# Attention and expert layers on one core: the last group's outputs expert by expert, part of the softmax inversions on GpSimd, and a new written order

## The chip, the cores and the metric

The kernel runs on one core of a Trainium2 chip. The core has five engines that work at the same time and each take their own instructions in program order: PE (TensorE, matrix products), DVE (VectorE), ACT (ScalarE), POOL (GpSimd) and SP (SyncE, which here only starts transfers). The metric is the device time of one execution in microseconds (us); lower is better.

## What is computed

Four batches of 1088 rows go through two layers. The first is a linear attention with sketched features: queries and keys (4 heads, 32 wide) are multiplied by two small random matrices, the outer product of the two sketches is the feature row, and the output is a ratio of two sums over the keys. Its output, four heads side by side, is the 128-wide input `x` of the second layer, four attention experts of which each row picks two:

```python
logits = x @ w_gate                      # 4 experts, the best 2 are kept
w = softmax over the two chosen logits
for e in range(E):
    scores = scale * (x @ wq[e]) @ (x @ wk[e]).T      # causal
    a = exp(scores - max); a /= a.sum(-1) + 1e-09
    ye = a @ (x @ wv[e]) @ wo[e]
    out += (expert e chosen for this row) * w * ye
```

All of it is float32, and the result must be the reference's.

## The kernel before, in words

**Tiles and stages.** A batch's 1088 rows are 17 blocks of 64 rows (index `i`), in three groups (`groups`, line 141): blocks 0 to 5, 6 to 11 and 12 to 16, so 384, 384 and 320 rows. As each row has two chosen experts, a block of 64 rows has 128 rows of scores. `prepare(b)` makes a batch's `x`: sketches (L518), their turn back on DVE (`back`, L522), products of sketches (`features`, one job for each head, on DVE or POOL, L527), sums over keys (L558), and from these `x`, twice: turned (`xT`) and as rows (`xra`, `xrb`, `xrc`, by way of DRAM). `choose_experts(b)` makes the masks of the chosen experts, also by way of DRAM.

For each group `queries` (L960, L969, L973) projects `x` for all four experts and picks the chosen ones by mask. For each block `scores` (lines 987 to 1054) runs a chain over four engines: PE multiplies (`score`, L998), DVE takes the scores with the causal mask and the row maximum (`take`, L1010), ACT exponentiates and adds up each row (`exp`, L1026), ACT or POOL adds 1e-9 to the sum (`guard`, L1032 or L1034), DVE inverts the 128 sums, one number in each partition (`invert`, L1037), POOL multiplies the block by the inverse and by the expert's share (`weigh`, L1041), DVE turns the block in squares of 32 (`turn A`, L1046). There are 68 such blocks. `values` (L1074) then sums over the keys for a whole group on PE, in two pairs of PSUM banks; the results are copied four times into `agg` (`keep V`, ACT or DVE), two of the copies are patched by mask (`patch V`, L1097, DVE), and POOL multiplies them by the masks in two instructions of two experts each (`spread V`, L1101). `outputs` projects `agg` with `Mo`: piece by piece of 128 rows, four experts for each piece (`project`, L1144), one copy to SBUF (`keep out`) and one store (L1157) for groups 0 and 1; all at once, turned (L1124, L1127) and stored in four transfers (L1130) for group 2.

**What sets the order.** Every such step is a job: a name, the engines it may run on with a price for each in us, what it reads, makes and holds. `ORDER` is a list of job numbers, written out; a letter behind a number picks the first (a, or none) or the second (b) engine of a job. `Plan.run` issues the jobs in just that order, so `ORDER` fixes the order on every engine and on the queues of the transfers, and, as buffers are taken from their pools in that order, also which buffer each tile gets. A job `dummy` multiplies a constant twice (L247) into a free pair of banks and feeds nothing; of 40 such jobs 6 are run, the others are left out. The last batch takes its groups in the order 1, 2, 0, so group 0 of batch 3 is the last work of the kernel.

PSUM is four pairs of banks (`ps`). `copy(eng, ...)`, line 191, is the line of every copy, whichever job makes it; in the profile such rows are told apart by their tiles and shapes.

Of the kernel before, what the change touches and what calls it, by code (L numbers as in the profile page):

```python
# [14 lines left out]
ALU = mybir.AluOpType  # L15
# [6 lines left out]
56 45 47 0 1 8a 77 60 46 3 2 76 25a 19a 17a 48 79 49 51 78 57 90 89 74 87 75 88 50 13b 98 100 99 102a 103a 91 92 83 93  # L22
97a 84 81 104b 22a 101b 113 96a 117 118a 82 111 112a 115 109 110a 94a 95a 38b 80 392 86 85 106 116a 393 114a 105 108a
107a 391 394 402 395 401 405 406 119 404 408a 54 120 124 125 129 407 130 121 66 122a 52 64 58 53 65 146 131 410a 126
411a 67b 132a 400 127a 147 152 55 68 397 396 69 123 71 150 70 148 153 155 44b 398 180 72 27b 16b 684 149 151 167 168
169 170 63 156 157a 158 685 159a 59 409b 179 184a 183a 154 162 163 181 399 185 73 182 413 412 186 414a 61 403 174 687
686 695 694 416 194 62a 415 417 195 196 420b 418b 215 216 419b 217 218a 421 222 423 9b 24b 31b 26b 422 164 219 171 128
165 137 187 188 133 172 246 173 430 431 197a 198 223 424 425 189 190a 191 245 250a 12b 166a 199 688 249a 201 202 200
318 5b 432 160 203 208 175 251 7a 426 427a 433a 224 247 192 428b 248 225a 161a 209 429 434a 210 252 319 322a 323a 193
435 698 268 226 227 700 699 204a 205 206 139 220 135 176 267 269 270 228 436 438a 207 141 703a 271b 704b 437b 324 221  # L30
211a 212 260 261 262 263a 213 275 321 276 277 278 279b 177 178b 214 253 254 456 458 272 457 273 14b 142 693 320 325
255 292 291 293 274 701a 42b 264 691 280 702a 134 136 229 230 231 459 460 692 256b 234a 284 294 283 233a 462 281 257
232a 258 265 690 689 706 705 285 286 235b 342 707a 708 237 236 239 709 710 696 713a 238 711a 712a 259 282 697 461 266
295a 296 343 326 344 297 287a 327 328 288 289 298 714 715 717 463 350 290 329 330b 716 723 724 725 345 346a 10b 143
21b 472 138 331 473 477b 718 347 351 352 35b 353 354a 144 727a 332 348 719 140 29b 439 476b 464 299 300 301 302 303
304 308a 441 306a 307a 726a 333 349 467 478 335 310 474 440 334 305b 309 475 336 479 359 337 338a 358 360 339 361 362
355 468 508 509 442 720a 984 311 312 540 721a 363 340 501 364a 443 502 480 979 341 481 482 541 314 465 487 365 488 356
357 483a 315 313 366 367 538 494 977 978 495 980 316a 981 728 539 542a 368 369 370 987 496 503 504a 145 371 372 373
374 317 469 375 470 543a 544 545 471a 505 506 985 988 484 485 486 497b 444 498 722 499 510 511b 489 490a 491 512 513
376 379b 447 500 380a 515 383 516 553 377a 381 445 554 492 493 378a 382 448 584 585 586 517 518a 729 555 449 446 453  # L40
982 983 730a 514 519 731b 451 991 520 521 993 749 556b 992 994b 587 588a 569 546 996b 750 384 385 997a 507 557 558 547
751 548 386 568 989 522 589 523 524 549a 550 551 559 570 571 526a 752 753 590 242 591 525a 754 611 529 995a 530 241
528b 527a 531 612 616a 561 760 732 452 387 615a 755 455 466 733 572a 756 560 573 574 389 614 562 563 986 613 240 576
577 617 618 620 575 43b 552 532 644 28b 18b 619 578 579 621 243a 580b 581 643 765 652 564a 565 766 769a 582 651 768
757 645 583 636 566 567 390 653 770a 771 635 654 655 627 622 244 623a 761 762 628 637 656 657b 629 630 638 767 772 624
658 659 646 625 592 660 639a 640 631b 641 593 594 450 595 596 597 794 598a 999 647a 632 642 601b 602 648 600a 599a 795
633 634 649 998 736 1000a 603 605 535 626 454 773 774 787 650 534 763 788 533 780 781 808 809 810 811a 764a 536b 812
661 662 789 775 663 813 796 797b 798 790b 604 782 664 665 666 667 1002 814 668 669 990 1005a 734 776b 777 672a 671a
778 1006b 670b 1001 735 739 1003 832 1004a 791 388 799 783b 800 673a 674 675 831 835a 801 784 1007 802 803 1008 792
676 1009 793 836a 834 677 1010 1016 833 904 738 678 742 30b 758 804b 1011 837 1017 785 805 806 759 1012 1018 838 1013a  # L50
905 908a 862 1014a 1020a 909a 807 679 910 878 786 779 737 537 877 879 747 839 840 841 907 906 880 911 861 863 1019a
1021 881b 842a 846 847 682 740 815 816 817 746 864 865a 820a 853 866 867 821a 824 854 1015 868 882 936 819a 823 39b
34b 40b 41b 855 848 849b 937 818a 850 851 856 822 938 1022 1024b 869 1023b 607 843 883 884 939 870 748 871 872 1042
857b 1044 928 680 741 681 844 845 1043 858 606 873a 874 929 608 1045 825 1047 852 930 940a 1046 1048 875 859 860 921
944 945 946 920 743 941 609a 922 610 744 913 931 932a 1049 912 914 947 933 934 942 915 948 876 949 950b 1126 916a 917
951 1125 1053 918 1054 1124 1128b 935 1025 1127 923 952 885 886 943 887 888 889 890 1129a 1051 891a 1130 1131 892b
924a 925 894b 895 828 896 926 898 893a 33b 927 32b 826 953 827 1139 829a 830 4 1147 1140 919 897 1055 1146 1132 1133
1148 1154 1155 1156 1198 1199 1149 1150a 1197 1201a 1134 1052 1027 1141 1142b 1143 1200 954 955 956 957 958 959 1202a
745 1029 1028 1026 1035 683 1037 960 1056 1057b 1135b 1157 1158b 1159 961 962 1203 1204 1213 1136 1137 1170 963a 1144
1145 1160 966a 1161 1171 1214 964a 968 1151 1152 1138 965a 967 1237 1205 1206 1172 1173 1174a 1238 1229 1215 970 969  # L60
1031 1207 1208 1209a 1239 1216 1059 1153 1039 1230 1162 1163 1217a 1240 1058 1231 1164 1061 1210 1211 1165 1241 1060
1063b 1050 1218 1062b 1166b 971 1064 1167 1175 1232 1242 899 1212 972 1168 1065 1176 1177 6b 1233a 1234 1169 1221
1243b 1040 1244 1222 1223 901 1235 1224 1066 900 1038 1067 1068 1245 1246 1219 1033 1069b 902a 1032 1030 1220 1101
1102 973 1178 1179 1034 1087 1225b 1226 1227 1236 1073 1074 1180 1075 1228 1088 1076a 1036 1181 1080 1081 1077 1094
1095 1096 1182 1103 1104b 1183 1184b 1097b 1098 1186b 1089 1090b 1091 1247 1248 1249 976 1187a 1105 1106 1250 1251
1252 1041 1188 1253 1254 1255 1185b 1189 1092 11b 1190 23b 903 1107 36b 1191 1194 1078 1070 1082 1083a 1193 1099 1093
975 1084 1071 1257b 1100 974 1192 1258a 1256a 1079 1085 1260 1261 1263 1259b 1086 1262 1072 1108 1195a 1196 1109 1110
1113a 1114b 1111a 1112b 1116 1117 1115 1264 1265 1267 1268 1266 1118 1120 1119 1121 1122a 15b 1269 1123 37b 20b
# [46 lines left out]
def kernel(  # L115
# [35 lines left out]
    def const(name, shape, dt=F32):  # L151
        return cp.tile(shape, dt, name=name, tag=name)
# [40 lines left out]
    def d_us(n):  # L193
        return 0.18 + n / 960

    def a_us(n):
        return 0.2 + 0.00073 * n

    def p_us(n):
        return 0.12 + 0.0022 * n  # L200
# [16 lines left out]
    warm = const("warm", [128, 1])  # L217
    den = const("den", [128, 2, 12])
# [16 lines left out]
    def first():  # L235
        nc.vector.memset(room(0, 64), 0)
        nc.vector.memset(warm, 0.0)

# [708 lines left out]
    def masks_of(b, n, *xs):  # L947
        return [("mb", b, n, x) for x in xs] if b == 0 and n == 0 else [("mb", b, n, 0)]
# [38 lines left out]
    def scores(b, n, i, rank):  # L987
# [48 lines left out]
        def invert():  # L1036
            nc.vector.reciprocal(rs[:, b, i : i + 1], rs[:, b, i : i + 1])  # L1037
# [13 lines left out]
        job(f"invert {b}.{i}", "DVE", 0.153, lambda e: invert(), [("zg", b, i)], ("r", b, i), rank=rank)  # L1051
# [4 lines left out]
    def values(b, n, rank):  # L1056
# [46 lines left out]
        r = rank + 0.1  # L1103
        for x in (2, 3, 0, 1):
            job(f"keep V {b}.{n}.{x}", ("ACT", "DVE"), (a_us(w), d_us(w)), lambda e, x=x: keep(e, x),
                [("V", b, n)], ("aggk", b, n, x), [Vk[x % 2], agg], rank=r)
# [3 lines left out]
        for x in range(2):  # L1110
            need = [("aggk", b, n, 0), ("aggk", b, n, 1)] if x == 0 else [("aggp", b, n)]
            job(f"spread V {b}.{n}.{x}", "POOL", p_us(2 * w), lambda e, x=x: spread_sums(x),
                [*need, *masks_of(b, n, x)], ("agg", b, n), [agg, mb], rank=r)

    def outputs(b, n, rank):
# [4 lines left out]
        if w % 128:  # L1120
# [15 lines left out]
            for g in range(4):  # L1136
                job(f"store out {b}.{n}.{g}", "SP", 0.5, lambda e, g=g: store_columns(g), [("ob", b, n)], None, [ob],
                    landing=0.35, rank=rank + 0.01)
            return
# [94 lines left out]
```

## Time and profile before

| | us |
|---|---|
| median of 3 runs | 280.45 |
| lowest and highest | 280.03, 280.90 |
| the profiled execution, as a run | 280.91 |
| its span, first to last instruction | 279.2 |
| around the span | 1.71 |
| busy: PE, DVE, POOL, ACT | 263.8, 218.8, 153.3, 100.2 |

The profile is one execution. Each row of a view is a group of instructions: the line, engine and operation, the tiles written and read with their shapes, how many, and their times. A float32 product of 128 x 128 weights is two records on PE, so 12 products are 24 rows. In the view by stretches of time, the numbers behind the stretch are the busy us of PE, PE's weight loads, DVE, ACT and POOL, then the granted PE clock (1.00 is full). In the timeline, `[5.76 <-issue]` is the time for which the engine stood idle before the row, and what ended it. The chain of work that ended last is followed back from the end: each piece is what the end was waiting for at that time.

### The profile page before, as it was taken

How to read it: one execution, taken by the hardware profiler on the slowest of the kernel's cores; microseconds unless marked ns; L12 is line 12 of the kernel's file. 1: busy time of each engine (PE TensorE's matmuls, PEld its weight loads, DVE VectorE, ACT ScalarE, POOL GpSimd, SP SyncE). 2: the span in 40 equal slices, each digit the busy share in tenths (PEclk: the TensorE clock that was granted, in tenths of full speed). 3: DMA queues.
4: the chain of work that ended last, by engine and by line, in shares of the span. 5: the costliest groups of instructions: out<-in, count | busy, mean ns of one | idle time of the engine just before them, and what ended most of it. 6: DMA issues, size and time to landing. Idle time of an engine off the chain costs nothing.

```text
span 279.2 us, 9471 instructions
## 1 busy us (share of the span) xinstructions
PE 263.8 (94%) x3953; PEld 194.8 (70%) x3953; DVE 218.8 (78%) x541; ACT 100.2 (36%) x272; POOL 153.3 (55%) x246
## 2 busy tenths in 40 slices
PE   5789899899999999989999999999999999999993
PEld 1478575448486796676589976756696975789973
DVE  4895998999989987998969437999898468986340
ACT  2030346254333444433462331463423335233110
POOL 6323636677789834546565458655447432544570
PEclk9979999999999999999999999999999999999999
DMA  8855749921617879243900166701403756820012
GB/s 179 139 141 102 112 124 258 153 34 24 143 32 120 166 184 180 57 102 65 198 6 4 30 150 141 162 2 38 108 2 76 130 116 133 165 56 5 2 31 52
DMA packets 85547, 27.36 MB, mean 98 GB/s; under 512 B 54080, under 2 KB 84864, under 8 KB 85504
## 3 DMA queue, kind: packets, MB, share of 16 engines
q1 hardware_dynamic: 83280, 26.47, 46.4%
q8 instruction: 31, 0.51, 0.8%
q10 hardware_dynamic: 2224, 0.28, 0.6%
q14 instruction: 12, 0.10, 0.1%
HBM read 22.22 MB, written 4.52 MB: 96 GB/s over the span
## 4 chain that ended last, share of the span: by engine, by line
PE 70%; DVE 20%; issue 5%; POOL 2%; ACT 1%; DMA 1%; DVEq 0%; POOLq 0%
PE pair L1074 24%; PE pair L998 19%; PE pair L960 9%; PE pair L1144 6%; PE pair L518 3%; PE pair L558 3%; DVE AT L1046 2%; DVE w L522 2%; DVE w L1010 2%; DVE fp L527 2%; PE pair L1124 2%; PE pair L615 1%; PE pair L592 1%; DVE in L494 1%; DVE xT L191 1%
## 5 line engine op out<-in xcount | busy, mean ns | idle before, releaser
L1041 POOL TENSOR_SCALAR w<-w,rs,sh 128x384 f32<-128x384 f32 (+15 forms) x68 | 55.6, 824 | 54.8 <-DVE rs L1037 52.0
L998 PE MATMUL pair<-xT,qs 128*128 128x384 f32 (+11 forms) x216 | 76.8, 482 | 1.7 <-DVE agg L191 1.3
L1026 ACT ACTIVATE w<-w,mx 128x640 f32<-128x640 f32 (+15 forms) x68 | 52.4, 770 | 72.3 <-DVE mx L1010 56.6
L998 PEld LDWEIGHTS pair<-xT,qs 128*128 128x128 f32 x216 | 37.7, 190 | 26.9 <-issue 10.0
L1046 DVE STREAM_TRANSPOSE AT<-w 128x576 f32<-128x576 f32 (+13 forms) x68 | 50.6, 758 | 5.4 <-POOL w L1041 5.2
L1010 DVE CUSTOM_DVE_ANT_0 w<-pair,mask 128x768 f32<-128x768 f32 (+13 forms) x68 | 48.3, 721 | 5.4 <-PE pair L998 4.7
L1074 PEld LDWEIGHTS pair<-AT,xra 32*128 32x128 f32 x1136 | 41.6, 185 | 6.0 <-DVE mx L1010 2.6
L1074 PE MATMUL pair<-AT,xra 32*128 32x192 f32 (+5 forms) x1136 | 44.5, 303 | 0.0
L1101 POOL TENSOR_TENSOR agg<-agg,mb 128x768 f32<-128x768 f32 (+1 forms) x24 | 37.3, 1565 | 12.7 <-ACT agg L191 6.6
L960 PE MATMUL pair<-xT,Mq 128*128 128x384 f32 (+1 forms) x96 | 34.9, 478 | 0.1
L527 POOL TENSOR_TENSOR fp<-w 128x576 f32<-128x576 f32 x21 | 25.4, 1224 | 14.2 <-DVE w L522 12.5
L191 ACT COPY agg<-pair 128x384 f32<-128x384 f32 (+1 forms) x33 | 14.0, 462 | 44.2 <-PE pair L1074 37.7
L1074 PE MATMUL pair<-AT,xrb 32*128 32x160 f32 (+5 forms) x752 | 26.9, 287 | 0.3 <-issue 0.3
L1074 PEld LDWEIGHTS pair<-AT,xrb 32*128 32x128 f32 x752 | 26.1, 186 | 1.0 <-issue 1.0
L1144 PEld LDWEIGHTS pair<-Mo,agg 128*128 128x128 f32 x192 | 23.4, 192 | 4.1 <-POOL agg L1101 1.7
L1144 PE MATMUL pair<-Mo,agg 128*128 128x128 f32 x192 | 24.9, 279 | 1.0 <-POOL agg L1101 0.9
L960 PEld LDWEIGHTS pair<-xT,Mq 128*128 128x128 f32 x96 | 17.2, 190 | 11.2 <-issue 3.2
L973 DVE COPY_PREDICATED qs<-mb,pair 128x768 f32<-128x768 uint16 (+1 forms) x24 | 23.0, 960 | 2.4 <-DMA mb<-md 1.8
L191 DVE COPY agg<-pair 128x384 f32<-128x384 f32 (+1 forms) x15 | 7.9, 532 | 13.1 <-PE pair L1074 11.7
L518 PE MATMUL pair<-in,SK 32*32 32x288 f32 x416 | 13.4, 494 | 3.0 <-DVE in L494 3.0
L522 DVE STREAM_TRANSPOSE w<-pair 128x576 f32<-128x576 f32 x16 | 11.6, 756 | 5.6 <-PE pair L518 5.6
L1097 DVE COPY_PREDICATED agg<-mb,pair 128x384 f32<-128x384 uint16 (+1 forms) x24 | 12.6, 550 | 3.3 <-ACT agg L191 2.9
(160 smaller groups left out, 295.4 us busy)
## 6 DMA issues: line engine op xcount, KB each, us to landing
mb<-md SPq DMA_DIRECT2D x7, 576.0 KB, 5.2
xra<-xd SPq DMA_DIRECT2D x16, 192.0 KB, 4.3
xrb<-xd SPq DMA_DIRECT2D x16, 192.0 KB, 3.6
xrc<-xd SPq DMA_DIRECT2D x16, 160.0 KB, 4.9
mb<-md SPq DMA_DIRECT2D x4, 480.0 KB, 5.4
in<-in_k_dram SPq DMA_DIRECT2D x12, 136.0 KB, 4.1
in<-in_q_dram SPq DMA_DIRECT2D x3, 544.0 KB, 5.5
xd<-w SPq DMA_DIRECT2D x12, 136.0 KB, 3.5
```

The costliest lines, as they stand in the source:

```text
L191: (nc.scalar.copy if eng == "ACT" else VEC[eng].tensor_copy)(o, i)
L527: VEC[e].tensor_tensor(out=f, in0=a[:, :, None, R : 2 * R].to_broadcast([128, NJ, R, R]), in1=a[:, :, 0:R, None].to_broadcast([128, NJ, R, ...
L960: nc.tensor.matmul(plan[ps[x]][:, y, 0:w], Mq[:, ((1, 2), (0, 3))[x][y]], plan[xT][:, 64 * t0 : 64 * t1], start=True, stop=True)
L973: nc.vector.copy_predicated(chosen(), rows(c), rows(plan[ps[x]]))
L998: nc.tensor.matmul(plan[p][:, y, 0 : c1 - c0], plan[qs][:, 128 * t : 128 * t + 128], plan[xT][:, c0:c1], start=True, stop=True)
L1010: nc.vector.tensor_tensor_reduce(out=o, in0=src, in1=msk, scale=-1.0, scalar=mx[:, b, i, x - 1 : x] if x else 3e38, op0=ALU.add, op1=ALU.m ...
L1026: nc.scalar.activation(out=a, in_=a, func=ACTF.Exp, bias=mx[:, b, i, last : last + 1], scale=-1.0, accum_out=zs[:, b, i : i + 1])
L1041: nc.gpsimd.tensor_scalar(out=a, in0=a, scalar1=rs[:, b, i : i + 1], scalar2=plan[("sh", b)][:, i : i + 1], op0=ALU.mult, op1=ALU.mult)
L1046: nc.vector.transpose(dst[:, 0 : keys // 32, t], plan[A][:, 0:keys].rearrange("p (j s) -> p j s", s=32))
L1074: nc.tensor.matmul(plan[Vk[g // 2]][:, g % 2, lo : 32 * nt], plan[(f"xr{j // 12}", b)][rows, j % 12], a[rows, j, lo:], start=(j == 0), sto ...
L1101: nc.gpsimd.tensor_tensor(out=a, in0=a, in1=plan[mb][:, 2 * x : 2 * x + 2, 0:w], op=ALU.mult)
L1144: nc.tensor.matmul(plan[p][0:m, 0, 128 * x : 128 * x + 128], plan[agg][:, e, 128 * x : 128 * x + m], Mo[:, e], start=(e == 0), stop=(e == ...
```

## The change

**The order.** `ORDER` is replaced as a whole by another list, with other choices of engine. The jobs are the same but for those below. Counted in the two lists, these move between engines:

| job | before | after |
|---|---|---|
| invert (softmax, 68) | DVE 68 | DVE 31, POOL 37 |
| features of queries | DVE 3, POOL 13 | DVE 9, POOL 7 |
| features of keys | DVE 8, POOL 8 | DVE 6, POOL 10 |
| base (copies of queries) | ACT 19, DVE 5 | ACT 16, DVE 8 |
| keep x (copies of x) | ACT 5, DVE 4 | ACT 8, DVE 1 |
| guard | ACT 39, POOL 29 | ACT 41, POOL 27 |
| keep V | ACT 33, DVE 15 | ACT 29, DVE 17 |
| keep w | DVE | ACT |
| scale of shares | POOL 3, DVE 2 | POOL 1, DVE 4 |

Of the six dummy jobs, four stood ahead of the first sketch, one behind the second sketch and one among the first batch's queries; in the new list one stands between the two first sketches, one among the first batch's later work and four behind the last output. On DVE, the first instructions `room` and `idle` change places.

**The inversion on POOL** is a new choice for the same job: the sum to the power of -1, with a constant tile `minus`. The plan's price for it is 0.555 us, against 0.153 us on DVE.

**The last group** (batch 3, group 0) gets its own jobs. `keep V` is left for two copies of four; the two others become `mix V`, in which DVE multiplies the PSUM sums by the mask straight into `agg`. The two-expert multiplications of POOL become one for each patched expert (`scale V`, POOL or DVE; the new list has one on each). The outputs are projected expert by expert, in the order 0, 2, 1, 3, three pieces for each, into three banks; each piece has its own copy and its own store, the stores from SP's or ACT's queue.

```diff
+    minus = const("minus", [128, 1])
...
         nc.vector.memset(warm, 0.0)
+        nc.vector.memset(minus, -1.0)
...
-        def invert():
-            nc.vector.reciprocal(rs[:, b, i : i + 1], rs[:, b, i : i + 1])
+        def invert(e):
+            r = rs[:, b, i : i + 1]
+            if e == "DVE":
+                nc.vector.reciprocal(r, r)
+            else:
+                nc.gpsimd.tensor_tensor(out=r, in0=r, in1=minus, op=ALU.pow)
...
-        job(f"invert {b}.{i}", "DVE", 0.153, ...)
+        job(f"invert {b}.{i}", ("DVE", "POOL"), (0.153, 0.555), ...)
...
+        if last_group(b, n):
+            def mix(x):
+                nc.vector.tensor_tensor(out=by_half(plan[agg][:, x]), in0=sums_of(x), in1=by_half(plan[mb][:, x]), op=ALU.mult)
+            def scale_one(e, x):
+                a = plan[agg][:, 2 + x, 0:w]
+                VEC[e].tensor_tensor(out=a, in0=a, in1=plan[mb][:, 2 + x, 0:w], op=ALU.mult)
+            for x in range(2):
+                job(f"keep V {b}.{n}.{2 + x}", ("ACT", "DVE"), ...)
+                job(f"mix V {b}.{n}.{x}", "DVE", ...)
+                job(f"patch V {b}.{n}.{x}", "DVE", ...)
+                job(f"scale V {b}.{n}.{x}", ("POOL", "DVE"), ...)
+            return
...
+    def last_group(b, n):
+        return b == B - 1 and n == 0
...
+        if last_group(b, n):
+            ps = [("ps", "po", b, n, x) for x in range(2)]
+            def piece(x):
+                return plan[ps[x // 2]][:, x % 2, 0:128]
+            def project_expert(e, first_, last_):
+                for x in range(3):
+                    nc.tensor.matmul(piece(x), plan[agg][:, e, 128 * x : 128 * x + 128], Mo[:, e], start=first_, stop=last_)
+            def keep_piece(e, x):
+                copy(e, plan[ob][:, 128 * x : 128 * x + 128], piece(x))
+            def store_piece(e, x):
+                (nc.scalar if e == "ACT" else nc.sync).dma_start(out=..., in_=plan[ob][:, 128 * x : 128 * x + 128])
+            order = (0, 2, 1, 3)
+            for y, e in enumerate(order):
+                job(f"out {b}.{n}.{e}", "PE", 12 * 0.056, ..., [("agg", b, n, e), ("M", 1)] + ([("po", b, n, y - 1)] if y else []), ...)
+            for x in range(3):
+                job(f"keep out {b}.{n}.{x}", ("ACT", "DVE"), ...)
+                job(f"store out {b}.{n}.{x}", ("SP", "ACT"), (0.45, 0.45), ...)
+            return
```

On the engines, the end of the new order reads: DVE keep V 2, patch 0, mix 0, mix 1, patch 1, turn out of group 2, scale 1, keep out 0, keep out 1; ACT keep V 3, keep out 2, store 2, store 0; POOL scale 0; PE out of group 2, then experts 0, 2, 1, 3, then the four dummy jobs; SP four stores of group 2, store 1.

114 lines of the change are left out of this document (66 added, 48 removed).

## The prediction

> **What bounds the kernel now.** I read the page first, then the stretches of time, then the end of the timeline, then single prices. The page says who is busy and what the end waited for:
>
> ```profile
> PE 263.8 (94%) x3953; PEld 194.8 (70%) x3953; DVE 218.8 (78%) x541; ACT 100.2 (36%) x272; POOL 153.3 (55%) x246
> PE 70%; DVE 20%; issue 5%; POOL 2%; ACT 1%; DMA 1%; DVEq 0%; POOLq 0%
> ```
>
> PE is the bound on average, DVE for a fifth of the chain. The average hides the stages, so I cut the span where the chain changes its engine:
>
> ```profile
> 0.00:12.00 12.00, 7.66 (x124) 3.81 (x136) 7.33 (x29) 1.52 (x2) 5.26 (x27) 1.00 0.79 161
> 12.00:24.00 12.00, 10.49 (x192) 7.44 (x165) 9.07 (x13) 2.94 (x7) 4.01 (x4) 0.86 0.50 111
> 24.00:56.00 32.00, 29.19 (x420) 19.38 (x419) 29.60 (x88) 12.96 (x40) 18.32 (x38) 1.00 0.83 163
> 56.00:86.00 30.00, 29.78 (x486) 20.54 (x486) 28.56 (x72) 12.11 (x33) 23.02 (x36) 1.00 0.31 62
> 190.00:268.90 78.90, 78.60 (x1196) 63.50 (x1195) 56.70 (x139) 27.78 (x74) 38.52 (x53) 1.00 0.37 76
> 268.90:279.20 10.30, 5.51 (x32) 4.14 (x32) 2.60 (x5) 1.34 (x3) 3.28 (x2) 1.00 0.16 35
> ```
>
> From 190 to 268.9 PE is idle for 0.3 us of 78.9: no reordering can win there, it can only lose. PE is idle for 8.7 us of the first 56, and for 4.8 of the last 10.3. So a gain has two places, the front and the end; everything between is PE work that the change leaves as it is (the same products, and six dummy jobs in both lists).
>
> **The end, step by step.** These rows follow the last sum over keys:
>
> ```profile
> 268.78 2.42 PE L1124 MATMUL pair<-agg,Mo 128*128 128x320 f32 x8
> 268.91 1.02 DVE L191 COPY agg<-pair 128x384 f32<-128x384 f32 x2 [3.30 <-PE pair L1074]
> 268.92 0.86 ACT L191 COPY agg<-pair 128x384 f32<-128x384 f32 x2 [2.66 <-PE pair L1074]
> 269.61 3.30 POOL L1101 TENSOR_TENSOR agg<-agg,mb 128x768 f32<-128x768 f32 x2 [1.88 <-ACT agg L191]
> 270.04 1.06 DVE L1097 COPY_PREDICATED agg<-mb,pair 128x384 f32<-128x384 uint16 x2
> 271.24 0.52 DVE L1127 STREAM_TRANSPOSE ob<-pair 128x320 f32<-128x320 f32 x1
> 271.30 0.71 PE L1144 MATMUL pair<-Mo,agg 128*128 128x128 f32 x4
> 272.96 2.50 PE L1144 MATMUL pair<-Mo,agg 128*128 128x128 f32 x20 [0.95 <-POOL agg L1101]
> 275.54 0.48 ACT L191 COPY ob<-pair 128x384 f32<-128x384 f32 x1 [5.76 <-issue]
> 276.04 0.39 SPq L1157 DMA_DIRECT2D out_dram<-ob  x1
> ```
>
> Copies, then 3.30 us of POOL in two halves; PE takes the first two experts of one piece at 271.30 and stands until the second half is done, runs 20 records in 2.50 and ends at 275.46. Call 268.9 T. After the change DVE does, one behind the other, a copy (0.51), patch 0, mix 0, mix 1, patch 1, the turn of group 2 (0.52, not before its product ends at T+2.3), scale 1. A mix has no row; it reads PSUM and a mask as a patch does, so I price it as the patch, the nearest row, 0.53 (1.06 for two); the ends are 0.43 (ACT's bare copy, 0.86 for two) and 0.82 (POOL's product for one expert, a quarter of 3.30). That puts mix 0 at T+1.6, mix 1 at T+2.1, patch 1 at T+2.7, the turn at T+3.2, scale 1 at T+3.8 (0.53 by the same row). POOL's scale 0 starts behind patch 0 at T+1.2 and takes the 0.82: T+2.0. PE's group 2 product still ends at T+2.3; 24 records at 0.125 (2.50 for 20) are 3.0, or 0.75 for each expert: expert 0 from T+2.3 (mix 0 ready since 1.6), expert 2 from 3.05 (ready since 2.0), expert 1 from 3.8 (since 2.1), expert 3 from 4.55 (since 3.8). PE no longer waits and ends at T+5.3, against 275.46 - 268.9 = T+6.56 before: **-1.25**. What is late next is PE itself.
>
> Behind it two of the three 128-wide copies are on DVE, one behind the other, one is on ACT with two stores queued behind it:
>
> ```profile
> L191 DVE COPY kvr<-pair 128x128 f32<-128x128 f32 x3 | 0.9, 288 | 2.3 <-PE pair L692 2.3
> 1.25 0.70 ACTq L233 DMA_DIRECT2D w<-in_S_dram  x1
> 1.31 3.59 PE L247 MATMUL pair<-idle 128*128 128x512 bf16 x8 [1.31 <-DVE idle L240]
> ```
>
> Copies are done 0.3 and 0.6 behind PE's end; ACT's second store begins 0.3 + 0.4 to 0.7 = 0.7 to 1.0 behind it, where the only store of before began 0.58 behind. It then moves a third of the bytes, 64 KB instead of 192. Before, the store's issue to the end of the span took 3.16 (276.04 to 279.2); the smaller transfer can be worth nothing or some half microsecond. I take +0.25 for the later start and -0.5 for the smaller piece: -0.25. The four dummy jobs behind the last output are at most 3.59 (eight records) from T+5.3, or from T+5.9 for the two that reuse a bank which the copies free, so they end at T+9.5 at the worst and T+7 at the record pace; the span now ends at T+10.3 and is forecast at T+8.8, so they are cover, and cost up to 0.7 only at the slow pace. **End: -1.5**, ends -0.5 and -2.
>
> **The inversions.** 37 leave DVE and come to POOL:
>
> ```profile
> L1037 DVE RECIPROCAL rs<-rs 128x1 f32<-128x1 f32 x68 | 8.9, 140 | 7.8 <-POOL rs L1034 5.9 <-ACT rs L1032 1.7
> 79.71 0.10 DVE L1037 RECIPROCAL rs<-rs 128x1 f32<-128x1 f32 x1
> 79.73 0.54 DVE L191 COPY qs<-pair 128x384 f32<-128x384 f32 x1
> L1034 POOL TENSOR_SCALAR rs<-zs 128x1 f32<-128x1 f32 x29 | 6.1, 211 | 15.3 <-ACT w L1026 12.3 <-ACT rs L1032 1.3
> POOL w L1041 <- DVE rs L1037: 52.0, 31, 5.8
> DVE AT L1046 <- POOL w L1041: 5.2, 5, 1.6
> L527 POOL TENSOR_TENSOR fp<-w 128x576 f32<-128x576 f32 x21 | 25.4, 1224 | 14.2 <-DVE w L522 12.5 <-DVE den L622 1.5
> ```
>
> A DVE inversion lasts 0.14, but the instruction behind it starts 0.02 later in the quoted pair, so 37 give DVE between 0.7 and 5.2, I take 0.07 each, 2.6. A power on POOL has no row: from 0.21 (the guard, same shape) to 1.22 (the longest product of two inputs); I take 0.555, the price that the plan writes for it, 20.5 us for 37. POOL waited 52.0 us in 31 places for a DVE inversion, 1.7 each; a power in POOL's own queue ends that wait for more than its price, and only 5 of 68 turns on DVE ever waited for POOL's block. So I cost POOL's part at nothing; POOL's idle 45% is the cover.
>
> **The front.** I counted the jobs that the first batch's second group of sums has ahead of it in both lists: it is the row at 78.46 of the timeline, and the DVE turn that frees its banks ends at 78.18. Below, the first five rows and the one at 0.99 are of the timeline, the two last ones pieces of the chain.
>
> ```profile
> 77.44 0.74 DVE L522 STREAM_TRANSPOSE w<-pair 128x576 f32<-128x576 f32 x1
> 78.46 4.18 PE L1074 MATMUL pair<-AT,xra 32*128 32x192 f32 x96
> 11.43 2.83 POOL L527 TENSOR_TENSOR fp<-w 128x576 f32<-128x576 f32 x2 [4.41 <-DVE w L522]
> 12.04 2.82 DVE L527 TENSOR_TENSOR fp<-w 128x576 f32<-128x576 f32 x2
> 16.26 2.77 DVE L527 TENSOR_TENSOR fp<-w 128x576 f32<-128x576 f32 x4
> L191 DVE COPY AT<-pair 128x768 f32<-128x768 f32 x1 | 0.9, 949 | 0.0
> L191 DVE COPY xT<-pair 128x512 f32<-128x512 f32 x4 | 4.3, 1120 | 0.1
> L191 DVE COPY agg<-pair 128x320 f32<-128x320 f32 x4 | 1.9, 487 | 8.1 <-PE pair L1074 6.7 <-ACT agg L191 1.4
> 0.99 0.27 DVE L240 MEMSET idle<- 128x256 uint32 x1
> 7.93 2.61 PE pair L518 x64
> 21.62 1.53 PE pair L518 x63
> ```
>
> Gone from DVE: 5 inversions (0.1 to 0.7), a copy of V (0.51), keep w (0.95), a keep x (1.12, with a small second copy up to 0.29), a tiny keep (up to 0.29): 2.7 to 3.9. New on DVE: two copies of queries (0.97), one 512-wide copy (0.51 to 0.95), one small one (up to 0.29): 1.5 to 2.2. Features: one of the first queries comes, two of the first keys go. Two on DVE took 2.82 while POOL ran its own two beside them, four took 2.77 alone; so the query stage becomes 1.41 + 0.69 + 0.69 = 2.8 with POOL's single one beside the first, and the key stage 2.82 for two beside POOL's two: both as before, I count 0, with 1.4 against it if POOL's copies disturb DVE too. Net -0.5 to -2.4, I take -1.3. Against it: the constant's fill now stands ahead of what the first loads wait for (0.27), and PE has two 448-wide scores ahead of it instead of two 384-wide queries (0.2). **Front: -0.8**, ends -2.4 and +1.4.
>
> In the Trainium skill, "GPSIMD Engine Reference", section "Key points", GpSimd shares its SBUF interfaces with VectorE, with contention when a DVE instruction has two SBUF inputs. The features rows agree (1.41 beside POOL, 0.69 alone). By that rule the five query features that come to DVE in later batches cost 1.41 rather than 0.69 each, 7.1 instead of 3.5, for which DVE, busy 218.8 of 279.2, has room behind the front; the sum stays 278.6 by either price.
>
> **The sum.** 280.9 (span 279.2 and 1.71 around it) - 1.5 - 0.8 = 278.6 for an execution like the profiled one. The median of the runs is 0.46 below that one, so the forecast is **278.2**.
>
> **Rivals.**
>
> *The middle takes it back (no change).* A new list has new tight places. PE had 0.3 idle in 78.9, so what was hidden is unseen; one stall like the 1.14 that PE has before 272.96, and the front's gain gone, is 278.2 + 0.8 + 1.1 = 280.1. For it: 37 inversions and, net, eight features change engine, and so every queue. Against: ahead of the second group of sums of batches 1 and 2 both lists have the same PE jobs but for dummies, and the new one has fewer DVE jobs.
>
> *POOL becomes late (slower).* Place: 56 to 86, where POOL is busy 23.02 of 30. Five powers of the first batch fall there. Its 7.0 idle us hold five powers of up to 1.4; from there on, each further 0.1 is 0.5 on DVE's turns and so on PE, and later batches add to it. At 2.2 us a power, that is 4.0: 278.2 + 4.0 = 282.2. Against: the nearest row, the guard of the same shape, is 0.21.
>
> *The change does more.* DVE's 7.8 us of waiting in front of inversions halve with their number. If the front's best end holds (-2.4 instead of -0.8) and a sixth of those 3.9 was on the chain, the time is 278.2 - 1.6 - 0.6 = 276.0.
>
> *The cold array (no change).* Four dummy jobs ahead of the first sketch go. The granted clock was 0.86 from 12 to 24, 1.7 us lost, and the first 64 sketch records took 2.61 against 1.53 at 21.62, in spite of the dummies, which had ended at 4.90. So they bought nothing that the rows show. If without them one more such stretch is slow, it is 278.2 + 1.7 = 279.9. In the Trainium skill, "TensorE: Matmul & The Clock Gate", Part 1, an idle array runs at half rate until a window of about 3.4 us has been busy, and falls back after an idle one; by that the three idle microseconds behind the dummies undo them, or, if the window falls otherwise, their loss costs a window, this rival.
>
> **How the numbers follow.** 0.3% (0.84 us) is about what a measurement of this kernel can tell from no change: faster is below 279.6, slower above 281.3. Forecast 0.49, more 0.13, middle 0.16, cold array 0.06, POOL late 0.16 with what features beside POOL add to it. Faster: the first two, 0.62. Same: 0.22. Slower: 0.16. The range leaves out most of POOL late and the far end of more: 275.7 to 281.5; it holds the bounds of the end (+1.0, -0.5) and of the front (+2.2, -1.6) about 278.2.
>
> **What would show it.** The end: PE's 24 records of the last group in one row that begins with the end of group 2's product, and 8.8 us instead of 10.3 from the last sum to the span's end. The inversions: the new POOL rows near 0.55 each, POOL's 52.0 of waiting for DVE's inversions about halved, the turns' 5.2 not grown. The front: the 96-record row earlier than 78.46 by about 0.8. The forecast is wrong if PE shows idle time between 86 and 268 where it had none, if a power takes over 1.4, or if the first sketch begins later than 7.93 by more than 0.3.

## The result, and the profile after

The changed kernel takes 281.8 us (median of 20 runs, 280.1 to 282.95) beside 280.07 of the kernel before: ratio 1.005, 95% interval 1.003 to 1.007. The forecast was 278.2. Its profiled execution is a run of 282.44 with a span of 280.7. Comparisons leave out a few executions of 287 to 288 us at a lower granted clock, three of them among the 12 of k1 below.

First, of the page of the changed kernel: busy time, the granted clock in 40 slices, and the chain of work that ended last.

```profile
PE 263.0 (94%) x3953; PEld 195.6 (70%) x3953; DVE 218.9 (78%) x515; ACT 101.8 (36%) x273; POOL 169.1 (60%) x274
PEclk9957999999999999999999999999999999999999
PE 57%; DVE 16%; POOL 10%; DMA 7%; issue 6%; ACT 2%; SPq 0%; DVEq 0%; POOLq 0%; ACTq 0%
```

PE's work is the same (263.0 against 263.8), but only 57% of the chain is PE, where it was 70; POOL has gone from 2% to 10%, DMA from 1% to 7%. The stretches of time, cut as before, say where:

```profile
12.00:24.00 12.00, 8.11 (x135) 7.14 (x132) 9.63 (x10) 1.54 (x3) 7.88 (x16) 0.60 0.36 84
24.00:56.00 32.00, 30.25 (x485) 20.19 (x485) 25.53 (x82) 13.42 (x42) 19.35 (x43) 0.99 0.85 156
190.00:268.90 78.90, 77.23 (x1180) 61.99 (x1180) 57.25 (x120) 28.55 (x73) 48.60 (x69) 1.00 0.38 78
```

From 12 to 24 PE is busy 8.11 instead of 10.49, at a granted clock of 0.60 instead of 0.86. From 24 to 56 it is busier than before (30.25 against 29.19). From 190 on it stands 1.67 where it stood 0.30. So the loss is in the front and near 230. The end itself, by the timeline; the first row is of the kernel before, the others of the changed kernel:

```profile
265.67 3.18 PE L1074 MATMUL pair<-AT,xra 32*128 32x192 f32 x92
...
269.01 3.18 PE L1081 MATMUL pair<-AT,xra 32*128 32x192 f32 x92
272.12 2.42 PE L1152 MATMUL pair<-agg,Mo 128*128 128x320 f32 x8
273.35 1.01 DVE L1113 TENSOR_TENSOR agg<-pair,mb 128x384 f32<-128x384 f32 x2
...
274.37 2.84 PE L1178 MATMUL pair<-Mo,agg 128*128 128x128 f32 x24
277.55 0.86 ACTq L1184 DMA_DIRECT2D out_dram<-ob  x2
```

The 24 records follow the group 2 product without a stop. From the end of the sums (272.2) to the span's end (280.7) it is 8.5 us, where it was 10.3. The end did what was forecast; everything ahead of it came 3.3 us late (the last sums begin at 269.01, before at 265.7).

### The profile page after: what moved, and what is told of

It reads as the page before. It is cut to its first block, busy times and chain, and to the rows that moved or that the text cites. A ratio compares the mean times of both kernels' runs of the same rounds, so it can differ in the third digit from the quotient of the medians.

```text
span 280.7 us, 9480 instructions
## 1 busy us (share of the span) xinstructions
PE 263.0 (94%) x3953; PEld 195.6 (70%) x3953; DVE 218.9 (78%) x515; ACT 101.8 (36%) x273; POOL 169.1 (60%) x274
## 4 chain that ended last, share of the span: by engine, by line
PE 57%; DVE 16%; POOL 10%; DMA 7%; issue 6%; ACT 2%; SPq 0%; DVEq 0%; POOLq 0%; ACTq 0%
PE pair L1081 19%; PE pair L1001 12%; PE pair L963 5%; PE pair L1202 5%; DMA mb<-md 4%; POOL w L1048 4%; DVE w L1013 4%; POOL agg L1108 3%; PE pair L1152 3%; PE pair L561 3%; PE pair L521 3%; DVE AT L1053 3%; DVE fp L530 2%; DVE qs L976 2%; DVE w L525 1%
## 5 line engine op out<-in xcount | busy, mean ns | idle before, releaser
L1001 PE MATMUL pair<-xT,qs 128*128 128x320 f32 (+11 forms) x216 | 75.5, 481 | 2.7 <-DVE qs L976 2.1
L1029 ACT ACTIVATE w<-w,mx 128x1088 f32<-128x1088 f32 (+14 forms) x68 | 52.4, 771 | 57.5 <-DVE mx L1013 46.1
L1048 POOL TENSOR_SCALAR w<-w,rs,sh 128x320 f32<-128x320 f32 (+15 forms) x68 | 56.0, 829 | 14.2 <-DVE rs L1042 10.1
L1053 DVE STREAM_TRANSPOSE AT<-w 128x256 f32<-128x256 f32 (+16 forms) x68 | 50.6, 759 | 8.6 <-POOL w L1048 8.3
L1013 DVE CUSTOM_DVE_ANT_0 w<-pair,mask 128x768 f32<-128x768 f32 (+14 forms) x68 | 47.7, 723 | 6.2 <-PE pair L1001 6.0
L1081 PE MATMUL pair<-AT,xra 32*128 32x160 f32 (+5 forms) x1136 | 43.8, 302 | 0.2 <-DVE AT L1053 0.2
L1108 POOL TENSOR_TENSOR agg<-agg,mb 128x768 f32<-128x768 f32 (+1 forms) x22 | 34.0, 1556 | 10.1 <-ACT agg L192 3.7
L1044 POOL TENSOR_TENSOR rs<-rs,minus 128x1 f32<-128x1 f32 x37 | 21.2, 575 | 24.1 <-ACT rs L1035 23.2
L530 POOL TENSOR_TENSOR fp<-w 128x576 f32<-128x576 f32 x17 | 20.9, 1240 | 9.7 <-DVE w L525 9.2
L976 DVE COPY_PREDICATED qs<-mb,pair 128x768 f32<-128x768 uint16 (+1 forms) x24 | 23.2, 966 | 1.9 <-DMA mb<-md 1.4
L1202 PE MATMUL pair<-Mo,agg 128*128 128x128 f32 x168 | 21.4, 278 | 0.3 <-ACT agg L192 0.3
L1037 POOL TENSOR_SCALAR rs<-zs 128x1 f32<-128x1 f32 x27 | 6.1, 226 | 23.1 <-ACT w L1029 21.7
```

Of the source, the lines that this page charges most:

```text
L530: VEC[e].tensor_tensor(out=f, in0=a[:, :, None, R : 2 * R].to_broadcast([128, NJ, R, R]), in1=a[:, :, 0:R, None].to_broadcast([128, NJ, R, ...
L976: nc.vector.copy_predicated(chosen(), rows(c), rows(plan[ps[x]]))
L1001: nc.tensor.matmul(plan[p][:, y, 0 : c1 - c0], plan[qs][:, 128 * t : 128 * t + 128], plan[xT][:, c0:c1], start=True, stop=True)
L1013: nc.vector.tensor_tensor_reduce(out=o, in0=src, in1=msk, scale=-1.0, scalar=mx[:, b, i, x - 1 : x] if x else 3e38, op0=ALU.add, op1=ALU.m ...
L1029: nc.scalar.activation(out=a, in_=a, func=ACTF.Exp, bias=mx[:, b, i, last : last + 1], scale=-1.0, accum_out=zs[:, b, i : i + 1])
L1048: nc.gpsimd.tensor_scalar(out=a, in0=a, scalar1=rs[:, b, i : i + 1], scalar2=plan[("sh", b)][:, i : i + 1], op0=ALU.mult, op1=ALU.mult)
```

## The experiments

The median of the kernel before lay between 279.85 and 280.37 in the five sets of runs, so differences between experiments are taken from the ratios to it: 0.001 is 0.28 us. A job is given with its engine behind an @; `spread` are GpSimd's multiplications by masks. e2m and m1m leave the 37 inversions out of what is computed.

| run | median us | ratio to before, 95% interval |
|---|---|---|
| e1: old order, new end | 278.31 | 0.9942 (0.9919 to 0.9964) |
| e2: e1 and 37 powers | 280.30 | 1.0002 (0.998 to 1.0024) |
| e2m: e2, products for powers | 278.44 | 0.9926 (0.9906 to 0.9945) |
| e3: new order, reciprocals | 293.09 | 1.0464 (1.0425 to 1.0503) |
| e4: dummy jobs first | 281.39 | 1.0054 (1.0032 to 1.0076) |
| d1: dummy jobs in the gap | 281.48 | 1.0048 (1.0026 to 1.0069) |
| s1: old front, new rest | 280.43 | 1.0015 (0.9993 to 1.0037) |
| s2: new front, old rest | 280.68 | 1.0026 (1.0 to 1.0053) |
| f1: features as in the old order | 279.06 | 0.9964 (0.9947 to 0.998) |
| q1: f1, query feature only | 281.59 | 1.0053 (1.0027 to 1.0079) |
| k1: f1, key features only | 279.98 | 1.0 (0.9981 to 1.0018) |
| m1: spreads ahead of a power | 279.80 | 1.0 (0.9977 to 1.0023) |
| m1m: m1, products for powers | 279.97 | 0.9974 (0.9951 to 0.9997) |
| c1: s1 and m1 | 277.91 | 0.9915 (0.9896 to 0.9933) |
| g1: f1 and m1 | 277.23 | 0.9901 (0.9882 to 0.9919) |
| a2: the changed kernel again | 281.09 | 1.0044 (1.0019 to 1.0068) |

### The end alone, and the powers in the old order (e1, e2, e2m, e3)

```diff
 # e1: the old list to the last sum, then the end of the new one
-keep V 3.0.0@ACT ... spread V 3.0.1@POOL, out 3.0.1, out 3.0.0, out 3.0.2, keep out 3.0.0@ACT
+keep V 3.0.2@DVE ... scale V 3.0.1@DVE, out 3.0.0, 2, 1, 3, keep out x3, store out x3
 # e2: e1, and
-invert@DVE x37
+invert@POOL x37   (at the same places of the list)
 # e2m: e2, and
-nc.gpsimd.tensor_tensor(out=r, in0=r, in1=minus, op=ALU.pow)
+nc.gpsimd.tensor_tensor(out=r, in0=r, in1=minus, op=ALU.mult)
```

> The old order of the work, with nothing changed but the last group's masked sums and outputs; all 68 inversions stay on DVE, the four dummy jobs stay ahead of the first sketch. Theory (the loss lies in the front of the new order, the new end is worth what was forecast): the end gains the 1.8 us that the two profiles show from the last sum to the span's end (10.3 before, 8.5 after), so about 278.3 us. Rival 1 (the new end gains only because everything ahead of it came late): 280.1, as before. Rival 2 (the end is worth my forecast of 1.5): 278.6, not told apart from the theory by more than 0.3.

> The old order with the new end, and of the 68 inversions the same 37 as in the changed kernel by GpSimd's power, each at the place that the inversion had in the old order. Theory (the powers cost nothing): within 0.3 of the run without them, so 278.3 us. Rival (the powers are what made the changed kernel late): 2 to 3 us above the run without them, 280.3 to 281.3.

> The old order with the new end and 37 inversions on GpSimd, but with a product in place of the power, so that these 37 inversions are left out of what is computed. The instruction has the same place, the same tiles and the same semaphores, and its expected duration is that of the nearest GpSimd rows of few columns, 0.21 to 0.24 us instead of 0.56. Theory (the price of the power is what costs 2.0 us in the old order, since GpSimd has no room from 78 to 87): 278.8 us or less. Rival (the place is what costs: the weighing now waits in GpSimd's own queue behind the sum): 280.3 as with the powers.

e1 is 1.6 faster than before (0.0058): the end is worth that by itself. e2 gives 1.7 of it back (0.0060): the powers are not free. e2m, with products at the same places that take 191 ns each, is back at e1. So the price of the power is what costs there, not its place. Below, the timeline of e1, then that of e2, near one of the places; e2 had begun its first sketch 0.5 earlier and was 0.66 ahead at 47.

```profile
47.76 0.59 PE L250 MATMUL pair<-idle 128*128 128x512 bf16 x2 [0.43 <-DVE qs L976]
...
80.46 1.18 POOL L530 TENSOR_TENSOR fp<-w 128x576 f32<-128x576 f32 x1
81.62 2.16 POOL L1048 TENSOR_SCALAR w<-w,rs,sh 128x832 f32<-128x832 f32 x2
85.60 0.98 DVE L976 COPY_PREDICATED qs<-mb,pair 128x768 f32<-128x768 uint16 x1
86.64 0.91 PE L963 MATMUL pair<-xT,Mq 128*128 128x384 f32 x2
```

```profile
47.10 0.59 PE L250 MATMUL pair<-idle 128*128 128x512 bf16 x2 [1.03 <-DVE qs L976]
...
80.50 1.10 POOL L1044 TENSOR_TENSOR rs<-rs,minus 128x1 f32<-128x1 f32 x2
81.56 1.18 POOL L530 TENSOR_TENSOR fp<-w 128x576 f32<-128x576 f32 x1
82.73 2.17 POOL L1048 TENSOR_SCALAR w<-w,rs,sh 128x832 f32<-128x832 f32 x2
86.03 0.98 DVE L976 COPY_PREDICATED qs<-mb,pair 128x768 f32<-128x768 uint16 x1
87.06 0.91 PE L963 MATMUL pair<-xT,Mq 128*128 128x384 f32 x2 [0.57 <-DVE qs L976]
```

Two powers, 1.10 us, push the feature product from 80.46 to 81.56 and the weighing from 81.62 to 82.73; DVE picks its queries later, and PE, which had not waited here, stands 0.57. These powers take 0.55 each, as predicted, but GpSimd has no room for them here, so they are not free. From 47 to 87 the lead of 0.66 has become a lag of 0.42.

The reverse, new order with reciprocals only:

```diff
-invert@POOL x37
+invert@DVE x37   (at their places in the new list)
```

> The changed kernel with its 37 powers put back on DVE as reciprocals, each at its place in the new order; nothing else. Theory (the powers cost nothing, the front does): 281.8 us as the changed kernel, within 0.5. Rival (the powers made it late): about 279.0 us or less, since 37 x 0.575 us leave GpSimd. Third possibility (the new order needs them on GpSimd): above 282.5.

293.09: the third possibility, far beyond what it named. The new list puts these inversions where GpSimd could wait for ACT's sum; a DVE that takes them in the same order waits there itself: by e3's waits DVE's inversions stand 10.3 us for ACT's sums (4.6 in the changed kernel), and GpSimd's weighing stands 60.7 for DVE's inversions (10.1). That this is the whole of the 12 us isn't shown. e3 tells that list and engines belong together, and nothing on the price of a power.

### Front or rest (s1, s2)

```diff
 # s1 (divide 0.2: the first batch's third ratio)
-new list to divide 0.2
+old list to divide 0.2   (then the new list's remaining jobs)
 # s2: new list to divide 0.2, then e1's remaining jobs
```

> The old order up to the third ratio of the first batch (the four dummy jobs ahead of the first sketch and the one between the sketches, query features on DVE and GpSimd two each, key features on DVE), about the first 27 us, and behind it everything else in the new order, with its 37 powers and the new end. Theory A (the new front is what made the changed kernel late): the front's 2.8 us of the profile, and with it the half-clock stretch, come back: 279.0 us. Theory B (the front is nearly made up by fewer stalls up to 126 us; the loss lies in the rest, in the powers and in the waits for masks): 281 or more, within 0.8 of the changed kernel.

> The reverse: the new order up to the third ratio of the first batch, and the old order behind it with all inversions on DVE, and the new end. Old front and old rest took 278.31. Theory A: 2.8 us more, 281.1. Theory B: within 0.8 of 278.3.

s2 is 2.35 above e1 (0.0084), near theory A: the new front costs that much before the same rest. s1 is 0.9 below the changed kernel (0.0047, the mean of the changed kernel's two ratios, less 0.0015), between the theories. Its profile is that of its slowest run (281.84) and shows a half-clock stretch, at 36 to 42 us (granted clock 0.86 from 32 to 56), that neither kernel's profile has and that I did not follow up, so s1 by itself decides nothing.

### What in the front (e4, d1, f1, q1, k1)

PE at the front of the kernel before, from its first turn of the query features on:

```profile
14.30 0.33 PE L592 MATMUL pair<-ident,fp 128*128 128x128 f32 x1 [0.85 <-POOL fp L527]
14.92 1.13 PE L592 MATMUL pair<-ident,fp 128*128 128x128 f32 x5 [0.29 <-DVE fp L527]
16.28 2.79 PE L592 MATMUL pair<-ident,fp 128*128 128x128 f32 x12 [0.23 <-DVE w L522]
19.00 2.62 PE L558 MATMUL pair<-vp,fp 128*64 128x33 f32 x72
```

PE at the front of the changed kernel, from its second sketch on, then DVE and GpSimd:

```profile
11.21 1.60 PE L521 MATMUL pair<-in,SK 32*32 32x288 f32 x64
15.64 3.25 PE L595 MATMUL pair<-ident,fp 128*128 128x128 f32 x14 [2.83 <-DVE fp L530]
19.95 4.06 PE L561 MATMUL pair<-vp,fp 128*64 128x33 f32 x72 [1.06 <-DVE fp L530]
```

```profile
11.92 3.66 DVE L530 TENSOR_TENSOR fp<-w 128x576 f32<-128x576 f32 x3
...
11.38 1.18 POOL L530 TENSOR_TENSOR fp<-w 128x576 f32<-128x576 f32 x1 [2.52 <-DVE w L525]
12.49 0.82 POOL L455 COPY vp<-w 64x128 f32<-64x128 f32 x1
13.26 1.05 POOL L452 COPY vp<-w 128x1024 f32<-128x1024 f32 x1
16.36 2.83 POOL L530 TENSOR_TENSOR fp<-w 128x576 f32<-128x576 f32 x2 [2.05 <-DVE w L525]
```

Three query features on DVE take 3.66, not 2.8. One by one they are 1.25, 1.82 and 0.74: the first ends at 13.17, 0.61 behind GpSimd's product (12.56), the second at 14.91, 0.60 behind GpSimd's copies of V (14.31), and the third has GpSimd idle beside it. So a feature on DVE seems to wait for the GpSimd instruction beside it, a copy as well as a product. PE stands 2.83 for the three. Then GpSimd waits 2.05 for the keys that DVE turns only behind its third feature.

The granted clock was 0.5 from 14.48 to 24.72, three windows of 3.41 us (an array at half pace is called cold here, and one that falls to it cools); in the kernel before it was one, from 16.35 to 19.77. The sums over keys begin 0.95 later than before (19.95 against 19.00) and take 4.06 at half pace instead of 2.62: together they end 2.4 later. In the Trainium skill, "TensorE: Matmul & The Clock Gate", Part 1, the clock goes by free-running windows of 3413 ns, and an idle one halves it. The trace agrees on the length, as the 10.24 us of the record are three such windows, but not on a window that is idle throughout: here the half pace came with a gap of 2.83, shorter than a window, and in the kernel before (twelve turns in 2.79) with gaps of 0.85, 0.29 and 0.23. First the dummy jobs:

```diff
 # e4
+dummy1 (behind idle), dummy15, dummy6, dummy23 (behind load q0.0) ... sketch q0
-dummy1, dummy15, dummy6 ... dummy23   (behind the last output)
 # d1
+dummy1, dummy15, dummy6   (behind sketch k0)
```

> The changed kernel with the four dummy jobs that stand behind its last output put where the old order had them, ahead of the first sketch; nothing else. Theory of the clock (without them the array is at half clock for three windows of 3.4 us, 14.5 to 24.7, instead of one): one half-clock window in the profile, and about 1.8 us less than the changed kernel's slower runs, 280.2 in nearly all runs. Rival (the dummies end three idle microseconds before the first sketch and do nothing; the gap of 2.8 us in front of the turn of the query features is what cools the array): three half-clock windows and 281.8 as the changed kernel.

> The changed kernel with three of the four dummy jobs from behind its last output put behind the second sketch, where PE is idle from 12.81 to 15.64 for the query features; they fill the gap and take nothing from the path if they end by 15.6. Theory (the idle gap lets the clock fall, and the sums over keys at 20 to 24 us then run at half pace): no half-clock window behind 15, sums over keys 2.6 instead of 4.06, about 280.3 us. Rival (the clock falls for the low activity of the weight-heavy turns and not for that gap): the half-clock windows stay and the time is 281.8, or up to 0.5 more if the dummies run late.

Neither moved the time: 1.0054 and 1.0048 beside 1.005 and 1.0044 of the changed kernel. My theory of e4 falls. (Its profile has two half-clock windows, but so has that of a2, the changed kernel again; the number differs from one execution to the next.) d1 is split: its profiled run had a granted clock of 1.00 from 12 to 24 and these rows:

```profile
15.24 1.77 PE L595 MATMUL pair<-ident,fp 128*128 128x128 f32 x14 [1.24 <-DVE fp L530]
19.54 2.29 PE L561 MATMUL pair<-vp,fp 128*64 128x33 f32 x72 [2.53 <-DVE fp L530]
```

So full pace is worth 1.5 on the turns and 1.8 on the sums, but the sums begin at 19.54 all the same, and in 8 of its 12 runs the mean granted clock was 0.994 or less. Those 8 took 280.86 to 281.99, the other four 279.65 to 280.61. Where the array cooled in the 8 no profile shows; the second gap is the likeliest place. Then the cause of the gaps, the engines of the first batch's features:

```diff
 # f1 (q1: the first pair of lines only; k1: the second only)
-features q0.0@DVE
+features q0.0@POOL                         (behind features q0.3@POOL, ahead of spread v1)
-features k0.0@POOL, features k0.1@POOL
+features k0.0@DVE, features k0.1@DVE       (behind features k0.2@DVE)
```

> The changed kernel with the engines of the first batch's features as in the old order: the third query feature on GpSimd ahead of its copies of V, the first two key features on DVE; nothing else. In the two profiles the first sum over keys began 0.95 later with the new split (19.95 against 19.00, both behind a first sketch that began within 0.12). Theory (the split is worth that part of the front, the half-clock stretch the rest): 0.9 less than the changed kernel, 280.9 us. Rival 1 (GpSimd's copies of V then come late and hold the sums up as long): 281.8. Rival 2 (the shorter gap also keeps the clock): 279.5.

> The changed kernel with only the third query feature of the first batch back on GpSimd, ahead of its copies of V; key features two and two as in the changed kernel. Theory (the query feature on DVE makes the gap ahead of the turns longer, 2.83 instead of 0.86 + 0.29, and lets the clock fall): most of the 2.7 us of the whole split, 279.5 us or less. Rival (the key features carry it): 281 or more.

> The changed kernel with only the two key features of the first batch back on DVE, query features three on DVE and one on GpSimd as in the changed kernel. Theory (the query feature carries the loss): within 0.5 of the changed kernel, 281.8 us. Rival (two key features beside each other at 1.41 each are slower than four on DVE at 0.76): 280.5 or less.

f1 is 2.3 faster than the changed kernel (0.0047 to -0.0036), all that s2 had put on the front and more than my theory's 0.9: its rival 2, that the clock is kept too, came true. The rows are those of f1, of q1 and of k1:

```profile
12.02 2.88 DVE L530 TENSOR_TENSOR fp<-w 128x576 f32<-128x576 f32 x2
...
14.34 0.33 PE L595 MATMUL pair<-ident,fp 128*128 128x128 f32 x1 [0.86 <-POOL fp L530]
14.96 1.66 PE L595 MATMUL pair<-ident,fp 128*128 128x128 f32 x13 [0.29 <-DVE fp L530]
17.96 2.67 PE L561 MATMUL pair<-vp,fp 128*64 128x33 f32 x72 [1.34 <-DVE fp L530]
```

```profile
14.59 1.66 PE L595 MATMUL pair<-ident,fp 128*128 128x128 f32 x13 [0.29 <-DVE fp L530]
19.47 3.48 PE L561 MATMUL pair<-vp,fp 128*64 128x33 f32 x72 [3.22 <-DVE fp L530]
```

```profile
15.77 2.67 PE L595 MATMUL pair<-ident,fp 128*128 128x128 f32 x14 [2.24 <-DVE fp L530]
18.68 2.80 PE L561 MATMUL pair<-vp,fp 128*64 128x33 f32 x72 [0.25 <-DVE fp L530]
```

The theory of q1 falls: with the query feature alone the turns come early, but PE then stands 3.22 for the keys, and the array cools there (3.48 for the sums). With the keys alone the first gap stays (2.24) and the second goes; that brings 1.3, so the theory of k1 falls as well. Only both together leave no gap above 1.34, and then the sums begin at 17.96 and take 2.67. In the changed kernel, q1 and k1 half pace followed the longest gap, but its length alone does not decide: d1 kept full pace behind 2.53 in its profile, and the kernel before fell to half pace behind 0.85, 0.29 and 0.23. By what rule gaps set the clock stays open.

### The wait near 230 (m1, m1m)

The chain of waits of the changed kernel, then rows of its timeline:

```profile
218.55 1.64 POOL agg L1108
...
221.71 1.65 POOL agg L1108
...
223.38 6.30 DMA mb<-md
```

```profile
218.01 0.57 POOL L1044 TENSOR_TENSOR rs<-rs,minus 128x1 f32<-128x1 f32 x1 [4.94 <-ACT rs L1035]
...
231.80 5.07 PE L1001 MATMUL pair<-xT,qs 128*128 128x448 f32 x12 [1.41 <-DVE qs L976]
```

Here a power (block 7 of batch 3) waits 4.94 us at the head of GpSimd's queue for ACT's sum. Behind it stand the two multiplications by masks of batch 2, whose inputs were there at 212.7. They end at 223.36, only then is their mask buffer free, the next masks are fetched into it in 6.30 us, and the queries wait for those: PE stands 1.41.

```diff
 patch V 2.1.1@DVE
+spread V 2.1.1@POOL, spread V 2.1.0@POOL
 ... shares 3.0@POOL ... invert 3.7@POOL
-spread V 2.1.1@POOL ... spread V 2.1.0@POOL
```

> The changed kernel with two GpSimd jobs moved: the two multiplications by masks of batch 2, group 1, stand ahead of the shares of batch 3 and of the power of its block 7, not behind them. In the changed kernel that power stood 4.94 us waiting for ACT's sum, the multiplications behind it ended at 223.36, only then was their mask buffer free for the next fetch of masks, which landed at 229.69, and PE was idle for 1.41. Theory (GpSimd's queue is blocked by a power whose own input is late, and the mask buffer carries that on to PE): the fetch is issued by about 220.5, the 1.41 goes, 280.4 us. Rival (the wait at 229 is only one of several late things): within 0.4 of the changed kernel's 281.8.

> The changed kernel with the two multiplications moved ahead (279.80 us), and again a product in place of each of the 37 powers, so that these inversions are left out. Theory (in the new order the powers cost nothing beyond the one blocked place): within 0.4 of 279.8. Rival (their 20.6 us on GpSimd still cost): 278.8 or less.

The multiplications in m1's timeline, and the last long stretch of m1:

```profile
211.74 3.25 POOL L1108 TENSOR_TENSOR agg<-agg,mb 128x768 f32<-128x768 f32 x2 [3.70 <-issue]
```

```profile
190.00:268.00 78.00, 77.74 (x1202) 62.42 (x1200) 57.02 (x118) 27.79 (x73) 48.82 (x68) 1.00 0.38 78
```

In m1 the multiplications run at 211.74, the fetch is issued at 219.38, and PE is idle 0.26 in the stretch. PE's rows are 1.1 ahead of the changed kernel's up to 226 and 2.6 ahead behind 232, so the move gains 1.5 there. The ratio falls by 0.0047, 1.3 us, as its theory had it. With products for the powers (m1m) it falls by a further 0.0026, 0.7 us, between the theory (0.4) and the rival (1.0), and the intervals overlap: in the new order most of the powers' price is covered, whether all of it isn't settled. This one queue was not covered.

### Both repairs (c1, g1), and the changed kernel again (a2)

```diff
 # c1: s1 and m1;  g1: f1 and m1;  a2: nothing changed
```

> Old front, new rest (280.43 us in its own run, beside 279.85 of the kernel before), and the two GpSimd multiplications moved ahead of the shares and the power, as in the run that moved these alone (279.80). Theory (front and blocked mask buffer are two separate losses of the changed kernel, together 3.4 of its 281.8): 278.5 us, as the old order with the new end (278.31). Rival (the new rest has further losses from the powers): 279.5 or more. If it is below 278.0, the new order's rest is worth something by itself.

> The changed kernel with both repairs: the first batch's features on the engines of the old order (alone 279.06 us) and the two GpSimd multiplications ahead of the shares and the power (alone 279.80, and 1.5 earlier behind 230 in the profile). Theory (two independent losses): 279.06 less 1.5, 277.5 us, the fastest of all. Rival (they share their gain, through the clock): 278.5 or more.

> The changed kernel itself once more, as the point of comparison on this chip: 281.8 us.

g1 takes 277.23 us, ratio 0.9901, less than either kernel: 4.1 below the changed one, where f1 and m1 add up to 3.6, so the two gains add up, as its theory had it (277.5). c1 gives 277.91; that the move is worth 2.8 there over s1 and 1.3 by itself I can't account for beyond s1's extra half-clock stretch. g1 is 1.15 below e1, and the intervals just touch, so with both repairs the new list looks better than the old one.

## Why the prediction was wrong, point by point

**The end: right.** Forecast -1.5; -1.8 in the profiles, -1.6 by e1. PE's 24 records stood in one row behind group 2's product, as written.

**The front: this step failed**, at "both as before, I count 0" for the features. Forecast was the row of 96 records 0.8 earlier than 78.46; it came 2.3 later, in the timeline of the changed kernel:

```profile
80.74 4.18 PE L1081 MATMUL pair<-AT,xra 32*128 32x192 f32 x96
```

The two stages were added up as durations of one engine: three features at 1.41 + 0.69 + 0.69. The copies of V that GpSimd runs behind its feature held up DVE's second one (1.82 where the sum has 0.69), which I had kept only as a bound of 1.4. The key features on DVE did take 2.83, as forecast, but began later. I did not put the two stages in a row: DVE's third feature holds the turn of the keys, and GpSimd's key features wait for that. And I gave a PE gap no price but its length. f1 shows these together at 2.3, where the sum has 0. The count that I went by, fewer DVE jobs, was no measure of any of this.

**The cold array: the mechanism came, from another cause.** I priced one more half-clock stretch at 1.7 and gave it 0.06, tied to the four dummy jobs. In the profile there were two more windows, and putting the dummy jobs back changed nothing (e4). The new split of features made the gaps, and without it the profiles of f1 and g1 show full pace from the turns on; that the gaps are what cools the array is argued from this, not shown gap by gap.

**The inversions: the price right, the cover wrong.** This is the second step that failed, at "I cost POOL's part at nothing". Of the changed kernel, first its group of powers, then two rows of its waits (what was waited for, us, times, longest):

```profile
L1044 POOL TENSOR_TENSOR rs<-rs,minus 128x1 f32<-128x1 f32 x37 | 21.2, 575 | 24.1 <-ACT rs L1035 23.2
```

```profile
POOL w L1048 <- DVE rs L1042: 10.1, 9, 2.1
DVE AT L1053 <- POOL w L1048: 8.3, 9, 2.3
```

A power takes 0.575 (taken: 0.555), and the wait of 52.0 fell to 10.1. But the powers themselves now wait 23.2 for ACT's sums, at the head of GpSimd's queue, and the turns' waiting grew from 5.2 to 8.3, which I had named as the sign against me. "POOL's idle 45% is the cover" is an average. In the old order it failed by price at 0.55 already (e2 against e2m, 2.1 us), where I had put the point at 1.4 per power; in the new order by one blocked place (m1, 1.3). The rival "POOL becomes late" names 282.2, near the 281.8 that was measured, but from powers of 2.2 us each; that the numbers are near is chance.

**The middle.** The rival that lets it take the front's gain back priced one stall at 1.1; there was one of 1.41. Against that, the remaining list gained some 0.7: +1.3 in all (the mean of the two ratios) is -1.6 for the end, +2.3 front, +1.3 near 230, and -0.7 that no run isolates. A likely place is 86 to 190, where PE stands 0.45 us in the changed kernel's profile and 1.47 in that of before.

## What to carry to other kernels

A wait of an engine's first instruction is a wait of all that stands behind it: before an operation goes to an engine with idle time, look at what is queued behind it and whose buffer that frees, not at the engine's share. Where two engines split a stage, write both queues down side by side to the next stage, and price a PE gap by its length and by the pace of what follows. A list of work that was fitted to one choice of engines can't be judged with another (e3).

## What the runs showed that I had not expected

The granted clock in the profile is not always the pace. In s2 the stretch from 16 to 20 shows 1.00, and so does the whole span, yet the turns and the sums run at the half pace of the changed kernel's rows, 3.25 and 4.06. The stretch, then the timeline of s2:

```profile
16.00:20.00 4.00, 3.23 (x14) 2.83 (x14) 3.96 (x4) 1.54 (x3) 3.29 (x3) 1.00 0.35 126
```

```profile
15.99 3.25 PE L595 MATMUL pair<-ident,fp 128*128 128x128 f32 x14 [1.75 <-DVE fp L530]
20.30 4.06 PE L561 MATMUL pair<-vp,fp 128*64 128x33 f32 x72 [1.06 <-DVE fp L530]
```

d1 has the same rows in 1.77 and 2.29. The durations of known rows are the better witness. And the 20 runs of the changed kernel fall into two heaps, spans of 278.4 to 279.3 and of 279.9 to 281.2; the first all have a mean granted clock of 0.994, the second in 8 of 11 runs 0.982 or 0.988. One window at half clock takes 0.006 off the mean over such a span (half of 3.41 in 280), so by the record the first heap has one window and those 8 runs two or three. Part of what a change to such a front is worth seems to be how often the windows fall badly: g1's five runs, with at most one by the record, lie within 0.5 us.
